# Reciprocal square roots of the q/k norm on VectorE instead of POOL, and a later place for the gain on kT

## Chip, cores, metric

One core of one Trainium2 chip. The time is the device time of one execution in microseconds; the median of several executions is compared.

## What is computed

Attention with RMS-normalised q and k, then a two-layer feed-forward with SiLU. All is fp32.

```python
# q, k, v: (8, 12, 448, 64); g_q, g_k: (64,); w_in: (768, 2048); w_out: (2048, 768)
rms = np.sqrt(np.mean(x * x, axis=-1, keepdims=True) + 1e-06)   # of q and of k
q_n, k_n = q / rms(q) * g_q, k / rms(k) * g_k
scores = np.matmul(q_n, k_n.transpose(0, 1, 3, 2)) / np.sqrt(64)
attn = softmax(scores)
x = np.matmul(attn, v)          # (B, H, S, D) -> (B*S, H*D) = (3584, 768)
h = x @ w_in
out = (h / (1 + np.exp(-h))) @ w_out
```

## The kernel before

**Couples.** Two pairs of heads (four heads of one batch entry) make a couple; there are NC = 24, numbered c = 0 to 23, six to a group of two batch entries (GROUP = 6). Each couple has a `visit(c)` and then a `between(c)`. In `visit` TensorE computes scores (L695, tile sc), ScalarE takes their exponentials (L700), TensorE multiplies the weights of the couple before and of this one with v (L732, tile av), and VectorE divides by the row sums while it copies out of PSUM (L790). A small copy of a constant into a bank of av (L708, `turn`) stands between two runs of L732 and orders them; inside a visit it is once VectorE's and once ScalarE's.

**Filler.** In `between` TensorE works on the feed-forward's first product of an earlier group: `begin` sets up the work, and each of two calls of `fill` per couple takes 13 or 14 matmul steps from it. It is a Strassen-Winograd scheme (class `Seven`): seven products of three steps each; the results leave PSUM through two banks (tile mm). Products 2, 6, 7, 3 and 4 are added up on VectorE (L816), products 1 and 5 are copied by ScalarE (L866, L876), and two sums of SBUF tiles are POOL's (`u2 += p5` at L878, and L879). The SiLU (L996) and the save of a row to `hidden` (L891, on SyncE's queue) follow. `fill` also deals out other work between the steps: `others` spread evenly, and `prompt`, whose first piece is issued at once and each further one after three more steps.

**Norm of couples c = 6 to 23.** `sum_squares` squares q or k on ScalarE into the buffer `squares` (L649) and sums groups of 32 on VectorE (L650). `scale` adds the two halves of a row by a matmul with `ident` (L662), makes mean + epsilon on VectorE (L663), raises it to -1/2 on POOL (L670: 28 columns for q, 28 for k) and multiplies the rows by it on POOL (L674). Couple c + 2 is scaled at the end of `between(c)`; c = 7 at the start of `between(6)`, and c = 6 in two halves in `between(4)` and `visit(5)`. The scaled rows are turned by VectorE in `flip`, q at L634 and k at L637. After k's turn ScalarE multiplies kT by the gains (L638), and the k load of couple c + 2 is issued to SyncE's queue. Couples c = 0 to 5 are normalised in another way (class `Norm`, L476), which the change leaves alone.

**Order.** Every engine runs its instructions in the order in which the code issues them; nothing is re-ordered, and waits between engines follow from the data. In the second `fill` of a couple `prompt` is: the first half of the row sums' reciprocals (L775), then the second half with its spreading by six DMAs (L781, L783), then `sum_squares(c + 2, "q")`. `flip(c + 1, "k")`, with L637 and L638, is issued before that fill.

**Weights.** w_in is loaded in pieces on SyncE's queue (L84), split by ScalarE (L99, L100), rounded by VectorE (L122, L125, L129) and added on POOL (L133). A load waits until the buffer of an earlier piece has been read by L133. Couples up to c = 10 do this beside everything else. VectorE also forms sums of w_in there (L813, L816).

**End.** After couple 23 the last group's feed-forward and the second product run (lines from L1165 on, tile alone).

Of the kernel before, what the change touches and what calls it, by code (L numbers as in the profile page):

```python
# [12 lines left out]
AF = mybir.ActivationFunctionType  # L13
ALU = mybir.AluOpType
AX = mybir.AxisListType
I32 = mybir.dt.int32
# [7 lines left out]


SCORE_MAX = 60.0

BANK = 512

# [160 lines left out]
def kernel(  # L190
# [161 lines left out]
    with tc.manual_schedule(), tc.tile_pool(  # L352
# [18 lines left out]
        for i in range(2):  # L371
# [9 lines left out]
        nc.vector.tensor_scalar(  # L381
            out=small, in0=most, scalar1=float(SCORE_MAX / D**0.5), scalar2=None, op0=ALU.is_le
        )
# [132 lines left out]
def bounded(  # L516
# [3 lines left out]
    P, D, R, J, S = z.P, z.D, z.R, z.J, z.S  # L520
# [6 lines left out]
    NC, loads, place, norm, spare, ones, first, squares = (  # L527
        own[name] for name in ("NC", "loads", "place", "norm", "spare", "ones", "first", "squares")
    )
    GROUP = z.NPAIR  # L530
# [13 lines left out]
    def piece(n):  # L544
        nonlocal at
        at += n
        return work[:, at - n : at]

    qT = piece(2 * S).rearrange("p (i s) -> p i s", i=2)
    kT = piece(z.NK)  # L550
# [13 lines left out]
    n = 2 * room.COLS  # L564
# [13 lines left out]
    def q_of(c):  # L578
        return rows_q[c % 2 if c < GROUP else 0]

    def load_q(c):

        if 0 < c < NC:
            loads["q"](c, raw_of(c) if c < GROUP else q_of(c))
# [32 lines left out]
    def transpose_k(c):  # L617


        assert z.KB == BANK  # L620
        t = ps.tile([P, 2, BANK], F32, name="sc", bufs=2)
        rows = place[f"k{c % 2}"]
        for i in range(2):
            for j in range(z.KEYS + 1 - i):
                nc.tensor.transpose(t[:, i, ts(j, P)], rows[:, ds((z.KA, z.KB)[i] + j * P, P)], ident)
        columns = t.rearrange("p i s -> p (i s)")[:, 0 : z.NK]
        nc.scalar.activation(kT, columns, AF.Copy, scale=gains)
        if c + 2 < NC:
            loads["k"](c + 2)

    def flip(c, name):

        if name == "q":
            nc.vector.transpose(qT.rearrange("p i s -> p (i s)"), q_of(c)[:, 0 : z.NK])  # L634
            load_q(c + 1)
            return
        nc.vector.transpose(kT, place[f"k{c % 2}"])  # L637
        nc.scalar.activation(kT, kT, AF.Copy, scale=gains)  # L638
        if c + 2 < NC:
            loads["k"](c + 2)  # L640

    n = z.NK // z.Q

# [11 lines left out]
    def scale(c, names="qk"):  # L655

        if c >= NC:
            return
        start = "qk".index(names[0]) * n
        f = norm.rms[c % 2][:, ds(start, len(names) * n)]  # L660
        t = ps.tile([P, 2, BANK], F32, name="sc", bufs=2)[:, 0, 0 : len(names) * n]
        nc.tensor.matmul(t, ident, f, start=True, stop=True)  # L662
        nc.vector.tensor_scalar(  # L663
            out=f, in0=t, scalar1=1.0 / D, scalar2=1e-6, op0=ALU.mult, op1=ALU.add
        )
        for i, name in enumerate(names):
            rows = q_of(c)[:, 0 : z.NK] if name == "q" else place[f"k{c % 2}"]
            rows = rows.rearrange("p (n e) -> p n e", e=z.Q)
            factor = f[:, ts(i, n)]
            nc.gpsimd.tensor_tensor(  # L670
                out=factor, in0=factor, in1=minus_half.to_broadcast([P, n]), op=ALU.pow
            )
            factor = factor.rearrange("p (n one) -> p n one", one=1).to_broadcast([P, n, z.Q])
            nc.gpsimd.tensor_tensor(out=rows, in0=rows, in1=factor, op=ALU.mult)  # L674

# [74 lines left out]
    def sum_up(c):  # L750

        n = D // 2
        early = c < GROUP
        t = bank(S) if early else ps.tile([P, 2, BANK], F32, name="sc", bufs=2)[:, 0, 0:S]
        terms = [(0, lambda: weights(c, 0))]
        if early:
            terms = [(0, lambda: weights(c, LEFT - 1))] + terms + [(1, None)]  # L760
        for k, (which, w) in enumerate(terms):
            if k == len(terms) - 2:
                yield
            for h in range(2):
                for i in range(2):
                    nc.tensor.matmul(  # L766
                        t[ds(h * D + i * n, n), :],
                        ones[:, which + i if which else 0],
                        eleft[:, h] if which else w()[:, i, h],
                        start=(k == 0), stop=(k == len(terms) - 1),  # L770
                    )

        def invert(half):
            rows = ts(half, S // 2)
            nc.vector.reciprocal(out=r[0][:, rows], in_=t[:, rows])  # L775

        def spread():
            mine = [a.rearrange("(h i p) s -> i h p s", h=2, i=2) for a in r]
            for i in range(2):
                for h in range(2):  # L780
                    nc.sync.dma_start(mine[1][i, h], mine[0][1, h])  # L781
            for h in range(2):
                nc.sync.dma_start(mine[0][1, h], mine[0][0, h])  # L783

        yield [lambda: invert(0), lambda: (invert(1), spread())]

    def divide(c, source):
        for i in range(2):
            x = x_of(c, i)
            nc.vector.tensor_tensor(  # L790
                out=x, in0=x if source is None else source[i], in1=r[i], op=ALU.mult
            )
# [136 lines left out]
    def sum_x(group, c):  # L929
        right_sums(*quarters(group, c), *sums_of_x(c))  # L930
# [128 lines left out]
    def take(n, *which):  # L1059

        for i in which or range(len(regions)):
            a, at = regions[i]
            if at + n <= a.shape[1]:
                regions[i][1] += n
                return a[:, ds(at, n)]
        raise AssertionError
# [10 lines left out]
    for at in ((1, 2), (2, 1), (2, 2)):  # L1077
        a = take(2 * z.HALF)
        results[at] = [a[:, ts(t, z.HALF)] for t in range(2)]
    a = take(2 * z.HALF)  # L1080
# [205 lines left out]
    def begin(work, columns, parts):  # L1286
        finish()
        filler.update(work=work, due=0.0, share=columns / parts)
# [31 lines left out]
    def finish():  # L1320
        run(filler["work"])
# [26 lines left out]
    def last_two(c):  # L1348
        return [c // GROUP * 2 - 2, c // GROUP * 2 - 1]

    def visit(c):
# [40 lines left out]
        if c == GROUP - 1:  # L1392
            scale(c + 1, "q")
# [18 lines left out]
    def run_all(work):  # L1412
        for piece in work:
            piece()

    def between(c):

        def transposes_and_sums():
            summing = sum_up(c)
            if c < GROUP:  # L1420
                next(summing)
            if c == GROUP:
                flip(c + 1, "q")
            if c < GROUP - 1:
                transpose_k(c + 1)
            elif c < NC - 1:
                flip(c + 1, "k")
            reciprocals = next(summing)
            if GROUP // 2 <= c <= EARLY:
                divide(c - 1, None)  # L1430
            return reciprocals

        if c < GROUP - 1:
            transpose_q(c + 1)
        elif c == GROUP:
            scale(c + 1)
        elif c < NC - 1:
            flip(c + 1, "q")
        if c < GROUP // 2:
            inverting.extend(transposes_and_sums())  # L1440
        elif c == GROUP - 1:
            run_all(transposes_and_sums())
        if c >= GROUP and c % GROUP == 0:
            fetched = range(AHEAD) if c == GROUP else ()
            columns = products - 2 * HW * S * len(fetched)
            work = halves_in(last_two(c), range(HF), plain_in, dict(begun), fetched)
            begin(work, columns, 2 * GROUP)
            begun.clear()
        late = add(c, LEFT - 1) + add(c, LEFT) if c >= GROUP else []
        keys = [lambda: sum_squares(c + 2, "k")] if c >= GROUP - 2 else []  # L1450
        queries = [lambda: sum_squares(c + 2, "q")] if c >= GROUP else []
        fill(late + weights_in(c, 0) + keys)
        prompt = transposes_and_sums() if GROUP // 2 <= c != GROUP - 1 else []
        if c == GROUP // 2:
            begin(make_ahead([0, 1]), AHEAD * 2 * HW * S, GROUP - 1)
        fill(weights_in(c, 1), prompt + queries)
        if c == GROUP - 2:
            pair_up()
            scale(c + 2, "k")
        elif c >= GROUP:  # L1460
            scale(c + 2)
        if c % GROUP == GROUP - 1:
            finish()
            if c == GROUP - 1:
                begun[0] = fetch_ahead([0, 1], 0)
            else:
                sum_x([c // GROUP * 2, c // GROUP * 2 + 1], 0)
        if GROUP <= c < NC - 1:

            nc.scalar.activation(first, minus_half, AF.Exp)  # L1470
        if c == NC - 1:
            while rounder.load():
                pass
# [236 lines left out]
```

## Time and profile before

| | |
|---|---|
| median of 3 runs | 1369.82 us (1369.28 to 1370.48) |
| profiled execution | 1367.72 us, of it 1365.9 us span |
| granted TensorE clock, mean | 0.989 |
| TensorE matmuls busy | 1301.1 us (95%) |
| VectorE busy | 956.5 us (70%) |
| ScalarE busy | 476.3 us (35%) |
| POOL busy | 445.5 us (33%) |

The profile is of one execution; its time lies 2.1 us below the median. In the views PE is TensorE, PEld its weight load, DVE VectorE, ACT ScalarE, POOL GpSimd, SPq SyncE's DMA queue. In a timeline a line gives start and duration in microseconds, the engine, the line of code, the operation, output<-input, the count, and in brackets how long the engine had been idle and what ended it. A group's line gives busy time, mean ns of one, and idle time with its releaser. A line of the waits view gives the waiting engine and line, what it waited for, then the total, the count and the longest.

### The profile page before, as it was taken

The page shows a single profiled execution, that of the slowest core. Times are in us where ns is not written, and L with a number is a line of the kernel's source. Part 1 is how long each engine was busy: PE and PEld are TensorE (multiplying, and loading weights), DVE is VectorE, ACT ScalarE, POOL GpSimd, SP SyncE. Part 2 cuts the span into 40 slices and gives each one's busy share as a digit, 9 for nine tenths or more (in the row PEclk, how much of TensorE's full clock was granted, in tenths as well). Part 3 has the DMA queues.
Part 4 walks back from the last instruction along what each step waited for, and adds up shares of the span by engine and source line. Part 5 has one row for each costly group of instructions (what it writes and reads, how often), then busy time and mean ns, then how long its engine had stood idle before and what let it go on. Part 6 is the DMA issues. An engine that isn't in the chain of part 4 may idle for free.

```text
span 1365.9 us, 19539 instructions
## 1 busy us (share of the span) xinstructions
PE 1301.1 (95%) x7113; PEld 818.2 (60%) x7113; DVE 956.5 (70%) x1595; ACT 476.3 (35%) x859; POOL 445.5 (33%) x241
## 2 busy tenths in 40 slices
PE   8997798888999999999999999999999999999998
PEld 4332343343444444444444455556999999999998
DVE  5785776675765555765554677679887787878785
ACT  7865263453544454444454234420000000000000
POOL 6755556554544544544542134330000000000000
PEclk9999999899999999999999999999999999999999
DMA  9564253522433343433331247531413232323311
GB/s 243 145 158 98 69 147 84 154 70 65 105 78 78 78 105 78 106 78 75 78 94 47 99 131 235 188 120 43 128 45 126 73 97 74 102 78 99 114 57 38
DMA packets 252558, 139.42 MB, mean 102 GB/s; under 512 B 190436, under 2 KB 236388, under 8 KB 252452
## 3 DMA queue, kind: packets, MB, share of 16 engines
q1 hardware_dynamic: 251888, 137.09, 35.9%
q8 instruction: 58, 0.95, 0.3%
q0 software_dynamic: 256, 0.79, 0.2%
q14 instruction: 48, 0.39, 0.1%
q10 hardware_dynamic: 308, 0.20, 0.1%
HBM read 88.47 MB, written 41.29 MB: 95 GB/s over the span
## 4 chain that ended last, share of the span: by engine, by line
PE 80%; DVE 7%; issue 4%; ACT 3%; DMA 2%; POOL 2%; SPq 1%; ACTq 0%; DVEq 0%; POOLq 0%
PE mm L858 23%; PE alone L1165 22%; PE sc L695 8%; PE av L732 8%; PE mm L1165 7%; PE alone L858 7%; PE alone L1202 2%; DVE work L746 2%; DVE work L775 1%; PE sc L766 1%; SPq L249 1%; ACT stage L996 1%; POOL rms L670 1%; PE mm L1202 1%; DVE rms L650 1%
## 5 line engine op out<-in xcount | busy, mean ns | idle before, releaser
L858 PE MATMUL mm<-x,W 128*128 128x448 f32 x636 | 262.7, 556 | 23.4 <-ACT stage L876 11.1
L858 PEld LDWEIGHTS mm<-x,W 128*128 128x128 f32 x636 | 118.1, 192 | 159.5 <-issue 114.0
L670 POOL TENSOR_TENSOR rms<-rms,minus_half 128x28 f32<-128x28 f32 x36 | 176.3, 4896 | 96.5 <-DVE rms L663 96.5
L858 PE MATMUL mm<-sums_x,W 128*128 128x448 f32 x456 | 190.2, 555 | 17.7 <-DVE stage L816 14.2
L746 DVE TENSOR_TENSOR work<-work 128x896 f32<-128x896 f32 (+1 forms) x114 | 138.8, 1242 | 46.6 <-PE av L732 46.1
L695 PE MATMUL sc<-work 64*64 64x448 f32 x1344 | 159.7, 543 | 1.2 <-ACT work L700 1.1
L732 PE MATMUL av<-work,rows 64*64 64x448 f32 x1296 | 148.6, 539 | 8.3 <-DVE x L790 2.7
L700 ACT ACTIVATE work<-sc 128x448 f32<-128x448 f32 x252 | 120.9, 542 | 97.4 <-PE sc L695 85.4
L858 PEld LDWEIGHTS mm<-sums_x,W 128*128 128x128 f32 x456 | 85.3, 193 | 115.7 <-issue 80.5
L503 POOL DMA_DIRECT2D out_dram<-x x2 | 1.3, 653 | 443.2 <-DVE x L816 443.2
L1165 PE MATMUL alone<-W,rows 128*128 128x192 f32 x608 | 113.0, 326 | 0.0
L878 POOL TENSOR_TENSOR parts<-parts,stage 128x448 f32<-128x448 f32 x31 | 42.0, 1356 | 209.8 <-DVE parts L816 209.8
L732 PEld LDWEIGHTS av<-work,rows 64*64 64x64 f32 x1296 | 53.0, 133 | 84.1 <-issue 37.2
L1165 PEld LDWEIGHTS alone<-W,rows 128*128 128x128 f32 x608 | 101.2, 190 | 0.0
L695 PEld LDWEIGHTS sc<-work 64*64 64x64 f32 x1344 | 51.5, 133 | 70.0 <-issue 34.1
L1165 PE MATMUL alone<-W,work 128*128 128x192 f32 x382 | 72.2, 326 | 0.0
L650 DVE TENSOR_REDUCE rms<-rows 128x28 f32<-128x896 f32 x36 | 38.7, 1076 | 44.3 <-ACT rows L649 44.2
L996 ACT ACTIVATE stage<-stage 128x896 f32<-128x896 f32 x63 | 57.2, 945 | 31.3 <-DVE stage L816 30.6
L674 POOL TENSOR_TENSOR rows<-rows,rms 128x896 f32<-128x896 f32 x36 | 64.4, 1790 | 2.8
L1165 PEld LDWEIGHTS alone<-W,work 128*128 128x128 f32 x382 | 63.8, 190 | 0.0
L1175 ACT COPY rows<-alone 128x192 f32<-128x192 f32 x34 | 10.8, 318 | 136.9 <-PE alone L1165 78.7
L775 DVE RECIPROCAL work<-sc 128x224 f32<-128x224 f32 x36 | 55.1, 1533 | 1.0 <-PE sc L766 1.0
(244 smaller groups left out, 2135.9 us busy)
## 6 DMA issues: line engine op xcount, KB each, us to landing
hidden<-stage SPq DMA_DIRECT2D x63, 448.0 KB, 2.8
work<-hidden SPq DMA_DIRECT2D x21, 1024.0 KB, 5.1
rows<-in_moe_w_out_dram SPq DMA_DIRECT2D x32, 384.0 KB, 3.4
W<-in_moe_w_in_dram SPq DMA_DIRECT2D x22, 512.0 KB, 5.0
work<-work SPq DMA_DIRECT2D x144, 56.0 KB, 1.9
rows<-in_q_dram SPq DMA_DIRECT2D x144, 56.0 KB, 2.2
rows<-in_k_dram SPq DMA_DIRECT2D x144, 56.0 KB, 2.2
x<-hidden SPq DMA_DIRECT2D x7, 1024.0 KB, 5.5
```

The costliest lines, as they stand in the source:

```text
L650: nc.vector.tensor_reduce(out=norm.rms[c % 2][:, ts("qk".index(name), n)], in_=squares.rearrange("p (n e) -> p n e", e=z.Q), axis=AX.X, op ...
L670: nc.gpsimd.tensor_tensor(out=factor, in0=factor, in1=minus_half.to_broadcast([P, n]), op=ALU.pow)
L674: nc.gpsimd.tensor_tensor(out=rows, in0=rows, in1=factor, op=ALU.mult)
L695: nc.tensor.matmul(two[ds(half * D, D), h, 0:S], keys[rows, ts(half, D)], qT[rows, pair, :], start=True, stop=True,)
L700: nc.scalar.activation(eleft[:, h] if j == LEFT else weights(c, j)[:, i, h], two[:, h, 0:S], AF.Exp, scale=norm.column(c, i, h, j) if c < ...
L732: nc.tensor.matmul(sums[i][ds(h * D, D), :], v, w, start=(j == 0 and step == 1), stop=(j == LEFT - 1 and step == 1),)
L746: nc.vector.tensor_tensor(out=total, in0=total, in1=more, op=ALU.add)
L775: nc.vector.reciprocal(out=r[0][:, rows], in_=t[:, rows])
L858: nc.tensor.matmul(t, self.left(name, s), self.right(name, s), start=s == ends[0], stop=s == ends[1])
L878: nc.gpsimd.tensor_tensor(out=u2, in0=u2, in1=p5, op=ALU.add)
L996: nc.scalar.activation(t, t, AF.Silu)
L1165: nc.tensor.matmul(t, x[:, i], y, start=i == ORDER[0], stop=i == ORDER[-1])
```

## The change

After L663, ten VectorE instructions compute the reciprocal square root in place: a start value from the bits of the number (one tensor_scalar on int32 views) and three Newton steps of three instructions each, with two stretches of `squares` as scratch. The two pows on POOL go; the two multiplications of the rows stay. The gain on kT is taken out of `flip` and becomes a piece of its own, the third of the prompt list, so that `sum_squares(c + 2, "q")` becomes the fourth. At c = 5 the list is issued as a whole, at once.

```diff
+RSQRT_START = float(0x5F375A86)
...
         nc.vector.transpose(kT, place[f"k{c % 2}"])
-        nc.scalar.activation(kT, kT, AF.Copy, scale=gains)
         if c + 2 < NC:
             loads["k"](c + 2)
+
+    def gain():
+
+        nc.scalar.activation(kT, kT, AF.Copy, scale=gains)
...
             out=f, in0=t, scalar1=1.0 / D, scalar2=1e-6, op0=ALU.mult, op1=ALU.add
         )
+        y, a = (squares[:, ts(i, len(names) * n)] for i in range(2))
+        nc.vector.tensor_scalar(
+            out=y.bitcast(I32), in0=f.bitcast(I32), scalar1=-0.5, scalar2=RSQRT_START,
+            op0=ALU.mult, op1=ALU.add,
+        )
+        for i in range(3):
+            nc.vector.tensor_tensor(out=a, in0=f, in1=y, op=ALU.mult)
+            nc.vector.scalar_tensor_tensor(
+                out=a, in0=a, scalar=-0.5, in1=y, op0=ALU.mult, op1=ALU.mult
+            )
+            nc.vector.scalar_tensor_tensor(
+                out=f if i == 2 else y, in0=a, scalar=1.5, in1=y, op0=ALU.add, op1=ALU.mult
+            )
         for i, name in enumerate(names):
...
-            nc.gpsimd.tensor_tensor(
-                out=factor, in0=factor, in1=minus_half.to_broadcast([P, n]), op=ALU.pow
-            )
             factor = factor.rearrange("p (n one) -> p n one", one=1).to_broadcast([P, n, z.Q])
             nc.gpsimd.tensor_tensor(out=rows, in0=rows, in1=factor, op=ALU.mult)
...
             reciprocals = next(summing)
+            if GROUP - 1 <= c < NC - 1:
+                reciprocals.insert(2, gain)
```

## The prediction

> **What bounds the kernel now.** I read the page first (busy shares), then the windows view by stage, TensorE's timeline for its gaps, and for each gap the timelines of the engines that it waited for.
>
> ```profile
> PE 1301.1 (95%) x7113; PEld 818.2 (60%) x7113; DVE 956.5 (70%) x1595; ACT 476.3 (35%) x859; POOL 445.5 (33%) x241
> ...
> L670 POOL TENSOR_TENSOR rms<-rms,minus_half 128x28 f32<-128x28 f32 x36 | 176.3, 4896 | 96.5 <-DVE rms L663 96.5
> ```
>
> TensorE is the bound over the whole span; POOL's pow (L670) is its largest single group, 4.9 us for 28 columns. Whether POOL ever holds TensorE is a matter of stage, so I cut the span (columns: us, then busy PE, PEld, DVE, ACT, POOL, then granted clock, DMA share, GB/s):
>
> ```profile
> 140.00:250.00 110.00, 90.28 (x425) 39.68 (x424) 76.86 (x94) 47.07 (x76) 61.75 (x27) 0.92 0.43 109
> 250.00:350.00 100.00, 89.69 (x493) 39.97 (x493) 70.81 (x83) 46.21 (x81) 57.12 (x23) 0.98 0.34 81
> 350.00:450.00 100.00, 97.54 (x524) 43.20 (x523) 62.50 (x76) 47.21 (x78) 48.37 (x19) 1.00 0.35 86
> ```
>
> From 350 us on TensorE is 98% busy at full clock: there little can be won. From 140 to 350 us (c = 6 to 11, the couples that still round w_in on VectorE and POOL) it is idle for 19.7 + 10.3 = 30 us, and the clock drops too. After 800 us no changed instruction runs. TensorE's timeline names the gaps:
>
> ```profile
> 162.23 4.19 PE L858 MATMUL mm<-sums_x,W 128*128 128x448 f32 x6 [6.71 <-DVE stage L816]
> ...
> 242.53 4.85 PE L858 MATMUL mm<-x,W 128*128 128x448 f32 x6 [7.88 <-ACT stage L876]
> ...
> 290.18 1.77 PE L858 MATMUL mm<-sums_x,W 128*128 128x448 f32 x4 [3.00 <-DVE stage L816]
> ...
> 321.61 6.47 PE L858 MATMUL mm<-sums_x,W 128*128 128x448 f32 x12 [2.05 <-ACT stage L866]
> ```
>
> The six matmuls after the two long gaps take 4.19 and 4.85 us where six take 2.42 elsewhere: a long gap costs about 2 us more in clock. For the first gap, POOL's timeline:
>
> ```profile
> 145.90 5.62 POOL L670 TENSOR_TENSOR rms<-rms,minus_half 128x28 f32<-128x28 f32 x1 [14.36 <-DVE rms L663]
> 151.60 1.88 POOL L674 TENSOR_TENSOR rows<-rows,rms 128x896 f32<-128x896 f32 x1
> 153.44 5.23 POOL L670 TENSOR_TENSOR rms<-rms,minus_half 128x28 f32<-128x28 f32 x1
> 158.74 1.70 POOL L674 TENSOR_TENSOR rows<-rows,rms 128x896 f32<-128x896 f32 x1
> 160.39 1.13 POOL L878 TENSOR_TENSOR parts<-parts,stage 128x448 f32<-128x448 f32 x1
> ```
>
> L878 (u2 += p5) had its inputs at 151.1 and stood behind the normalisation until 160.4; VectorE's L816 waited for it until 161.56 ("7.53 <-POOL parts L878") and TensorE for L816. The second gap is the same queue one step removed: POOL's rounding add L133 stood behind pow until 224.03, and SyncE's load of w_in behind L133:
>
> ```profile
> SPq L84 <- POOL W L133: 40.0, 4, 19.6
> ```
>
> SyncE stood until 226.19; with it the v and q loads and the save of the hidden row (issued 239.11), whose landing L876 waited for until 241.95. The other two gaps are ScalarE's and VectorE's order: L638 (the gain on kT) waits on L637, and copies out of PSUM stand behind it:
>
> ```profile
> ACT work L638 <- DVE work L637: 92.7, 18, 15.3
> ```
>
> At 321 us L866 ran at 321.04, directly after L638, some 2 us after its product was done.
>
> **What the Trainium skill says.** "VectorE: DVE Perf Modes", TRN2 errata, gives fp32 tensor_tensor (N+151)/0.96 ns. The trace agrees: 691 ns by formula for 128x512 (rows 681 to 691), 624 for 448 (L790 624). "GPSIMD Engine Reference", Key points: POOL contends with VectorE instructions that run in a two-port mode or have two SBUF inputs. Here L125 took 1.80 us beside L674 (427 ns alone) and L746 2.13 (1.09 alone), but L816 with a PSUM operand 0.58 to 0.62 beside L674. "TensorE: Matmul & The Clock Gate", Part 1, has the array fall to half clock after some 3.4 us idle: the 4.19 and 4.85 us above fit. No row of this trace shows a 56-column tensor_tensor.
>
> **Part 1: pow out of POOL.** 36 pows go, 176.3 us, 9.8 us per couple. On VectorE come 10 instructions after each of the 19 L663. With 56 columns: the tensor_scalar about 0.19 us (L472, 8 to 14 columns, 0.171), nine others (56+151)/0.96 = 0.216 us, 2.13 us busy; all depend on the one before, and dependent pairs here start 0.035 us after the end (L122 231.03+0.43, L125 231.50), so the chain is 2.48 us. The two 28-column calls: 2.2 us. VectorE's load rises by 17 x 2.13 + 2 x 1.85 = 40 us. Bounds for one instruction: 0.171 (L472) to 0.35 (128x192 rows): chain 2.1 to 3.9 us.
>
> Where it lies: in 16 couples (visits 7 to 22) the chain falls between L663 and L708, the write into an av bank that TensorE needs next:
>
> ```profile
> 399.48 0.22 DVE L663 TENSOR_SCALAR rms<-sc 128x56 f32<-128x56 f32 x1 [0.23 <-PE sc L662]
> 401.95 0.16 DVE L708 COPY av<-minus_half 128x1 f32<-128x1 f32 x1 [2.25 <-PE av L732]
> ```
>
> VectorE is idle there for 2.25 us. The weight load behind L708 starts at 402.16 and its matmul at 402.43, back to back with the scores ahead of it, so 0.14 us more are free: 2.39 against 2.48, 0.1 us late, x 16 = 1.6 us. L790 behind L708 waits for TensorE until 403.45 and is not moved; it has one SBUF operand, so L674, now beside it, should leave it alone. At c = 7 and 11, POOL still runs L878/L879 beside the chain: about 0.9 us each, 1.8 us. POOL then scales q 4.3 us after L663 instead of 6.6, and k after 6.0 instead of 13.1; the transposes L634 and L637, 10 to 20 us later, don't notice, except at c = 5 (L634 waited 1.59 us: gain 1.6). The scratch y, a is in `squares`: its next Square is a fill later (at c = 6, 148.97, when the chain ends at about 148.4).
>
> Gains, gap by gap:
> - c = 6 (142 to 175). The chain delays the first evacuation (146.74) by 2.5 us, and TensorE's next product with it. L674 ends at about 152 instead of 160.3, the evacuation of product 7 at about 155, L878 at 156.2, L816 at 157.3; TensorE goes on at 158.5 instead of 162.23 and keeps its clock: 3.7 + 1.8 = 5.5 us. With the 1.6 us above: 7.1.
> - c = 8 (210 to 255). L674 ends at 216.6, so L125 is done at 217.05, L129 at 217.8, L133 at 219.1 instead of 226.1: SyncE goes on 6.9 us earlier, the row's save is issued at about 232.3 and landed at 235.2; TensorE runs dry at 234.6. The gap shrinks from 7.88 to about 1.2: 6.7, clock 2.4, and most of 0.47 + 0.81 (L746 beside L133): 9.5 us.
> - c = 9, 10: 0.60 at 268 (L746 beside L674), 1.22 and 1.63 at 309 and 313 (L133 and L878 behind pow): 3.4 us.
>
> **Part 2: the gain moved.** One ScalarE instruction, 1.04 us, no DMA. It goes from just after L637 to the sixth matmul step of the second fill; the k load (8 DMAs on SyncE) stays directly behind L637, so that queue isn't touched. Scores need kT some 5 us after that (step 14), so it is hidden; at c = 5 nothing of ScalarE lies between old and new place. It passes L99/L100, L866 or L876, and the silus. What it pushes: the Square of q and its reduce L650 go from step 6 to step 9, on VectorE past one evacuation. TensorE's L662 needs L650 at step 13 or 14, 3 us later, and Square plus L650 take 2.1: hidden.
> - c = 10: the 2.05 at 321 and its slow clock (6.47 against 4.67 for 12): 3.5 us.
> - c = 9: at 290 L816 stood behind L650, which waited for Square: 3.0. c = 7: p5's copy behind the gain, 0.6 of 1.21. c = 6: p5's copy behind Square, 1.05.
> - c = 14, 17, 20 (430.71, 534.05, 638.30): the same L816 behind L650, 0.78 each: 2.3.
>
> Sum: 7.1 + 9.5 + 3.4 + 3.5 + 3.0 + 0.6 + 1.05 + 2.3 = 30.5 us. Against it 1.6 + 1.8, and one term that I choose: per couple c = 7 to 10 VectorE is busy 27 to 30 us of the 33 that a couple takes without gaps (c = 11: 32.8), and goes to over 90%, so a fifth of the 26 us won before 350 us is likely to come back as other waits: 5. Net 22 us. From the profiled 1367.7 (span 1365.9 and 1.8 around it) that is 1345.7; the median is 2.1 higher, so 1348.
>
> **The rivals.**
> - *Slower: the chain outlasts VectorE's gap ahead of L708.* Its price is (chain - 2.39) in 16 couples. It eats 26 us from a chain of 4.0 us, 0.40 us an instruction. For it: every instruction depends on the last, none of this size is in the trace, and POOL may stretch them. Against: formula and rows put it at 2.5. At 0.45: 16 x 2.1 = 34 less 26, 1378. Chance 0.10.
> - *Cover elsewhere: VectorE becomes the bound in c = 6 to 11.* POOL's L674 and L133 now fall into VectorE's busy stretches, and the w_in stalls return as L816 waits; only the c = 8 gap and half the rest go: about 10 us, 1360. Chance 0.20.
> - *No change*, gains and late L708 cancelling (chain near 3.5 to 4): 0.05.
> - *Forecast*: 0.65, 1338 to 1356.
>
> I count 0.2% (2.7 us) as what a measurement here can tell from no change. Faster 0.85, same 0.05, slower 0.10. The range 1336 to 1364 takes in the forecast and the second rival, and leaves out the rest.
>
> **What would show it.** Right: no L670 rows; ten VectorE rows of about 0.2 us a call; SyncE's L84 wait on L133 far under 40 us; gaps at about 158 and 235 under 3 us; clock in 140:250 near 1.0; L708 waits under 0.3 us each. Wrong: TensorE's av waits on L708 of a us or more per couple, or the stage from 140 to 350 us as long as before.

## The result, and the profile after

| | before | changed |
|---|---|---|
| median | 1369.66 us (1369.28 to 1371.83, six runs) | 1363.72 us (1362.40 to 1364.75, six runs) |
| profiled execution, span | 1367.72, 1365.9 us | 1364.28, 1362.5 us |

The ratio is 0.9953, interval 0.994 to 0.9966: 5.9 us faster, where 22 were forecast. Of the runs told below one, of the kernel with the gain alone, took 1528.04 us at a mean granted clock of 0.844 where its five others had 0.991 or more; it is left out of that kernel's ratio, and the median told below, 1361.16, would be 1360.20 without it.

Lines below are the changed kernel's unless another kernel is named; they have moved on by 5 to 15. L663 is now L668, the chain is L672 to L681, POOL's multiplication L674 is L689, L708 is L723, L732 is L747, L746 is L761, L790 is L805, L813 is L828, L816 is L831, L858 is L873, L866 and L876 are L881 and L891.

The page of the changed kernel, its line of busy times and the group of POOL's multiplications:

```profile
PE 1302.9 (96%) x7113; PEld 818.6 (60%) x7113; DVE 991.2 (73%) x1785; ACT 475.7 (35%) x859; POOL 266.2 (20%) x205
...
L689 POOL TENSOR_TENSOR rows<-rows,rms 128x896 f32<-128x896 f32 x36 | 62.7, 1762 | 143.9 <-ACT work L715 49.2
```

POOL has lost 179 us and 36 instructions, VectorE has gained 35 us and 190: the change did what it says. The windows of the changed kernel, with the columns of the prediction's table:

```profile
140.00:250.00 110.00, 100.30 (x500) 43.48 (x494) 90.27 (x143) 53.59 (x88) 33.03 (x23) 0.96 0.48 125
250.00:350.00 100.00, 93.85 (x490) 42.05 (x486) 79.12 (x108) 47.64 (x80) 25.43 (x18) 1.00 0.35 81
350.00:450.00 100.00, 94.23 (x510) 41.77 (x502) 66.50 (x103) 44.41 (x75) 18.51 (x12) 0.98 0.33 82
```

From 140 to 350 us TensorE is busy for 14 us more than before, and the clock has risen from 0.92 and 0.98 to 0.96 and 1.00. But the third row, where it had been 97.54 busy at full clock, has lost 3.3 us and some clock. The gaps of TensorE's timeline say why:

```profile
150.88 4.78 PE L873 MATMUL mm<-x,W 128*128 128x448 f32 x12 [0.85 <-DVE parts L831]
157.13 1.02 PE L873 MATMUL mm<-sums_x,W 128*128 128x448 f32 x2 [1.47 <-DVE parts L831]
...
165.74 4.22 PE L873 MATMUL mm<-sums_x,W 128*128 128x448 f32 x6 [2.41 <-DVE stage L831]
...
233.70 4.13 PE L873 MATMUL mm<-x,W 128*128 128x448 f32 x6 [2.56 <-ACT stage L891]
...
357.63 1.77 PE L747 MATMUL av<-work,rows 64*64 64x448 f32 x8 [5.11 <-DVE av L723]
...
569.96 1.77 PE L747 MATMUL av<-work,rows 64*64 64x448 f32 x8 [5.21 <-DVE av L723]
571.51 3.21 PE L710 MATMUL sc<-work 64*64 64x448 f32 x16
```

At c = 8 the 7.88 us of before have become 2.56. At c = 6 the gap of 6.71 us is gone from its place, but three waits of 0.85, 1.47 and 2.41 us stand elsewhere in the couple. Two gaps of over 5 us are new, and each takes clock with it: eight av matmuls take 1.77 us behind it and 0.98 in the kernel before, sixteen score matmuls 3.21 and 1.85. Both gaps lie at the entry of a visit that follows a group's last couple (c = 12 and 18), and there VectorE's queue looks like this:

```profile
352.01 0.62 DVE L831 TENSOR_TENSOR stage<-mm,parts 128x448 f32<-128x448 f32 x1
352.54 1.86 DVE L828 TENSOR_TENSOR sums_x<-x 128x448 f32<-128x448 f32 x1
354.43 2.00 DVE L828 TENSOR_TENSOR sums_x<-x,sums_x 128x448 f32<-128x448 f32 x1
356.35 0.61 DVE L828 TENSOR_TENSOR x<-x 128x448 f32<-128x448 f32 x1
356.89 0.61 DVE L828 TENSOR_TENSOR sums_x<-x,sums_x 128x448 f32<-128x448 f32 x1
357.42 0.15 DVE L723 COPY av<-minus_half 128x1 f32<-128x1 f32 x1
```

At 352.01 the chain has just ended. At c = 11 and 17 the code issues, behind `scale`, the last copy of a product out of PSUM (an evacuation, L831) and four sums of x (`sum_x` of part 0), and only then L723. No instruction there waits: VectorE is simply full. The two L828 of 1.86 and 2.00 us run beside POOL:

```profile
352.22 3.73 POOL L689 TENSOR_TENSOR rows<-rows,rms 128x896 f32<-128x896 f32 x2 [4.51 <-issue]
```

The same place in the timeline of the kernel before:

```profile
365.14 0.61 DVE L816 TENSOR_TENSOR stage<-mm,parts 128x448 f32<-128x448 f32 x1
365.67 0.61 DVE L813 TENSOR_TENSOR sums_x<-x 128x448 f32<-128x448 f32 x1
...
367.93 0.15 DVE L708 COPY av<-minus_half 128x1 f32<-128x1 f32 x1
```

L708 is over at 368.08, and TensorE's next av matmul starts at 368.14: it was just in time, with nothing to spare.

### The profile page after: what moved, and what is told of

Same layout as the page of the kernel before. It is cut to its first block, busy times and chain, and to the rows that moved or that the text cites. A ratio compares the mean times of both kernels' runs of the same rounds, so it can differ in the third digit from the quotient of the medians.

```text
span 1362.5 us, 19714 instructions
## 1 busy us (share of the span) xinstructions
PE 1302.9 (96%) x7113; PEld 818.6 (60%) x7113; DVE 991.2 (73%) x1785; ACT 475.7 (35%) x859; POOL 266.2 (20%) x205
## 4 chain that ended last, share of the span: by engine, by line
PE 64%; DVE 2%; DMA 1%; SPq 1%; ACT 1%; issue 0%; POOL 0%; ACTq 0%; DVEq 0%; POOLq 0%
PE alone L1180 22%; PE mm L873 17%; PE mm L1180 7%; PE alone L873 7%; PE sc L710 4%; PE av L747 4%; PE alone L1217 2%; PE mm L1217 1%; PE sc L781 1%; DVE sums_x L828 0%; DMA hidden<-stage 0%; SPq L251 0%; DVE work L831 0%; DMA work<-work 0%; POOL parts L893 0%
## 5 line engine op out<-in xcount | busy, mean ns | idle before, releaser
L873 PE MATMUL mm<-x,W 128*128 128x448 f32 x636 | 258.6, 549 | 13.8 <-ACT stage L891 5.2
L873 PEld LDWEIGHTS mm<-x,W 128*128 128x128 f32 x636 | 117.6, 191 | 147.5 <-issue 111.9
L873 PE MATMUL mm<-sums_x,W 128*128 128x448 f32 x456 | 187.2, 549 | 7.4 <-DVE stage L831 4.4
L747 PE MATMUL av<-work,rows 64*64 64x448 f32 x1296 | 152.1, 552 | 20.9 <-DVE av L723 15.4
L710 PE MATMUL sc<-work 64*64 64x448 f32 x1344 | 163.7, 558 | 2.2 <-ACT work L715 2.0
L761 DVE TENSOR_TENSOR work<-work 128x896 f32<-128x896 f32 (+1 forms) x114 | 128.6, 1153 | 51.1 <-PE av L747 46.0
L873 PEld LDWEIGHTS mm<-sums_x,W 128*128 128x128 f32 x456 | 84.9, 191 | 102.3 <-issue 80.9
L747 PEld LDWEIGHTS av<-work,rows 64*64 64x64 f32 x1296 | 53.0, 135 | 98.2 <-issue 39.4
L689 POOL TENSOR_TENSOR rows<-rows,rms 128x896 f32<-128x896 f32 x36 | 62.7, 1762 | 143.9 <-ACT work L715 49.2
L881 ACT COPY stage<-mm 128x448 f32<-128x448 f32 x27 | 14.3, 531 | 130.2 <-PE mm L873 130.1
L790 DVE RECIPROCAL work<-sc 128x224 f32<-128x224 f32 x36 | 55.1, 1533 | 1.0 <-PE sc L781 1.0
```

Of the source, the lines that this page charges most:

```text
L710: nc.tensor.matmul(two[ds(half * D, D), h, 0:S], keys[rows, ts(half, D)], qT[rows, pair, :], start=True, stop=True,)
L747: nc.tensor.matmul(sums[i][ds(h * D, D), :], v, w, start=(j == 0 and step == 1), stop=(j == LEFT - 1 and step == 1),)
L761: nc.vector.tensor_tensor(out=total, in0=total, in1=more, op=ALU.add)
L873: nc.tensor.matmul(t, self.left(name, s), self.right(name, s), start=s == ends[0], stop=s == ends[1])
```

## Where the time went, couple by couple

TensorE's row-sum matmul (L662 before, L667 after) marks the end of a couple. The table gives the change of each stretch's length against the kernel before, in us, read from one profiled execution of each kernel. The forecast's column is its own steps put in their places, ahead of its discount of 5. The last three kernels are experiments told below.

| stretch | forecast | changed | gain moved only | Newton only | chain in the visit |
|---|---|---|---|---|---|
| up to c = 6 | -1.6 | +2.7 | +2.2 | -1.5 | -1.5 |
| c = 6 | -6.6 | -3.7 | -2.9 | -3.1 | -3.7 |
| c = 7 | +0.4 | -1.4 | +0.8 | +2.8 | -0.2 |
| c = 8 | -9.4 | -6.4 | -0.6 | -6.5 | -5.7 |
| c = 9 | -3.5 | -4.3 | -3.3 | -0.8 | -4.3 |
| c = 10 | -6.2 | -3.1 | -2.1 | -0.7 | -3.1 |
| c = 11 | +1.0 | +0.6 | 0.0 | +0.6 | +0.6 |
| c = 12 | +0.1 | **+5.8** | 0.0 | **+5.7** | +2.3 |
| c = 13 to 17 | -1.1 | -1.1 | -1.3 | -0.1 | -1.3 |
| c = 18 | +0.1 | **+7.2** | 0.0 | **+6.6** | +2.3 |
| c = 19 to 21 | -0.5 | -0.7 | -0.7 | -0.2 | -0.8 |
| sum | -27.3 | -4.5 | -7.8 | +2.9 | -15.3 |

Up to c = 12 the changed kernel and the last one issue the same instructions, and yet the first row differs by 4.2 us: that much the early part varies from one execution to another, and it is no effect of an edit. A difference of a us in one cell of c = 6 to 8 is no more than that either (c = 7: -1.4 and -0.2 with the same instructions). From c = 6 to 11 the changed kernel gained 18.3 us; the forecast had 24.3 there less its discount, 19. What the forecast did not have are the 13.0 us of c = 12 and 18.

## The experiments

Every ratio is against the kernel before, timed on the same chip with the kernel named; medians move by a us or two between chips, so ratios are compared.

**Each part alone.** One kernel moves the gain and leaves pow on POOL (the two edits are shown against the changed kernel):

```diff
+            nc.gpsimd.tensor_tensor(
+                out=factor, in0=factor, in1=minus_half.to_broadcast([P, n]), op=ALU.pow
+            )
...
-        y, a = (squares[:, ts(i, len(names) * n)] for i in range(2))
-        nc.vector.tensor_scalar(
...
```

> Only the later place of the gain; the reciprocal square root stays POOL's pow. Theory A (the change's lost time sits at the two group ends, c = 12 and 18, where the chain and POOL's multiplications now hold L723 behind four sum_x; the gain's move is nearly free): 6 to 10 us faster than before, from the gaps at 290 (3.0), 321 (3.5) and the three of 0.78, with L84 still waiting 40 us on L133 and no new wait on L723. Theory B (the gain's move does little, the c = 6 to 11 gains all come from POOL): under 3 us.

The other has the chain on VectorE and leaves the gain behind the turn:

```diff
         nc.vector.transpose(kT, place[f"k{c % 2}"])
+        nc.scalar.activation(kT, kT, AF.Copy, scale=gains)
...
-            if GROUP - 1 <= c < NC - 1:
-                reciprocals.insert(2, gain)
```

> Only the chain on VectorE in place of pow; the gain stays directly behind L639. Theory A: the gaps at 162 and 242 shrink by 3 to 6 us each, and 10 to 13 us are lost at c = 12 and 18 (L723 waits of about 5 us): within 3 us of before. Theory B: faster by 4 us or more, about what the whole change won (5.9).

The gain's move alone took 1361.16 us against 1368.57, ratio 0.9946 (0.9931 to 0.9961). It alone is worth what the whole change brought. The chain alone took 1372.04 against the same 1368.57, ratio 1.0031 (1.0021 to 1.0042): the part that clears POOL made the kernel slower. Its TensorE timeline at c = 12:

```profile
364.05 1.77 PE L745 MATMUL av<-work,rows 64*64 64x448 f32 x8 [5.12 <-DVE av L721]
```

With the gain alone there is no gap at c = 12 or 18 (the table). So the loss belongs to the chain's part. The effects of the two parts roughly add up: by the table -7.8 and +2.9 against -4.5, by the ratios -7.4 and +4.2 against -6.4, where the difference of 3 us is as wide as the three intervals together allow.

**Taking the loss away.** Two kernels change only the group ends. One issues POOL's two multiplications of couples 13 and 19 behind the next visit's division:

```diff
+        if c % GROUP == 1 and c > GROUP + 1:
+            return
+        multiply(c, names)
...
         if c == GROUP - 1:
             scale(c + 1, "q")
+        if c > GROUP and c % GROUP == 0:
+            multiply(c + 1)
```

> The changed kernel, with only POOL's two multiplications of c = 13 and 19 put behind the division of the next visit; the chain stays ahead of the four sum_x. If POOL's contention with sum_x makes a good half of the wait on L723 there: the wait falls from 5.1 to about 2.5 us twice, and the time is 4 to 6 us under the changed kernel (ratio to before 0.991 to 0.993). If the chain's own 2.5 us make nearly all of it: under 2 us gained.

It took 1361.53 us, ratio 0.9946 (0.9934 to 0.9959). That looks like 1 us or so gained, but its POOL timeline shows that the edit moved nothing:

```profile
350.82 3.73 POOL L699 TENSOR_TENSOR rows<-rows,rms 128x896 f32<-128x896 f32 x2 [4.52 <-issue]
```

The chain ended at 350.7 there. POOL has its own order, nothing of POOL's stood between the old and the new place, and no data of VectorE's later work is asked for; so the multiplications began where they had begun, and the gap at c = 12 was 5.12 us. The run tells nothing of the two causes. The other kernel issues the chain there too, only the mean (L668) staying behind:

```diff
                 divide(c - 1, sums)
                 run_all(beside[1:2])
+                if c > GROUP and c % GROUP == 0:
+                    root(c + 1)
```

`root` is the chain and the two multiplications; `scale` leaves it out for these two couples:

```diff
+        if c % GROUP == 1 and c > GROUP + 1:
+            return
+        root(c, names)
```

> The changed kernel, with chain and multiplications of c = 13 and 19 put behind the division of the next visit. Theory A: L723 is on time at c = 12 and 18, and 10 to 13 us come back, less what the chain costs behind the division: ratio to before 0.986 to 0.989 (1350 to 1354). Rival (the lost time is spread over all couples, as late L723 or VectorE as the bound in c = 6 to 11): within 3 us of the changed kernel.

It took 1355.05 us, ratio 0.99 (0.9885 to 0.9916), 13.5 us under the kernel before and faster than both kernels. In its VectorE timeline the four sums are unstretched and L723 (here L733) follows them at once. The last of them, and L733:

```profile
349.52 0.62 DVE L838 TENSOR_TENSOR sums_x<-x,sums_x 128x448 f32<-128x448 f32 x1
350.05 0.15 DVE L733 COPY av<-minus_half 128x1 f32<-128x1 f32 x1
```

and TensorE goes on at 350.26. The gain is 3.5 us at c = 12 and 5.0 at c = 18 of the table, not the whole loss, because something else is late next in the same couple:

```profile
364.81 2.52 PE L883 MATMUL mm<-sums_x,W 128*128 128x448 f32 x6 [1.69 <-ACT stage L891]
```

**How much is the chain, how much POOL's multiplication.** Both kernels start from the one with the gain alone. The first adds a chain whose result nobody reads, with pow and so the multiplications where they were:

```diff
+        y, a = (squares[:, ts(i, len(names) * n)] for i in range(2))
+        nc.vector.tensor_scalar(out=y.bitcast(I32), in0=f.bitcast(I32), ...)
+        for i in range(3):
+            nc.vector.tensor_tensor(out=a, in0=y, in1=y, op=ALU.mult)
...
```

> The kernel with the gain moved and the power kept on POOL, plus ten VectorE instructions of the chain's kinds and sizes at the chain's place, whose result nobody reads. It adds the chain's length to VectorE's queue; POOL's multiplications stay where the power puts them, some ten us later than in the changed kernel. Theory A (at the two group ends the late L723 has two equal halves: the chain's own 2.5 us, and two L828 that POOL's multiplications stretch by 1.3 us each): L723 is 2.2 to 2.6 us late at couples 12 and 18, no L828 is stretched, and the time is 5 to 8 us above the kernel with the gain alone (1361), so 1366 to 1369. Theory B (the chain lies in idle time of VectorE there too, and the multiplications make the whole 5 us): L723 in time at both ends, 1361 to 1363.

The second multiplies the rows of couples 13 and 19 by one ahead of the pow, with no chain:

```diff
+        if c % GROUP == 1 and c > GROUP + 1:
+            one = squares[:, 0:1]
+            nc.vector.tensor_scalar(out=one, in0=f[:, 0:1], scalar1=0.0, scalar2=1.0, ...)
+            for rows in (q_of(c)[:, 0 : z.NK], place[f"k{c % 2}"]):
...
+                nc.gpsimd.tensor_tensor(out=rows, in0=rows, in1=factor, op=ALU.mult)
```

> The kernel with the gain moved and the power kept on POOL; for couples 13 and 19 alone, POOL first multiplies q and k by one (in the same form as L689, 3.7 us in all, the ones written by one small VectorE instruction behind L668), so that it runs beside the L828 of the group ends. No chain. Theory A: two L828 take 1.8 to 2.1 us in place of 0.62, L723 is 2.3 to 2.9 us late at couples 12 and 18, and the time is 4 to 6 us above the kernel with the gain alone (1361): 1365 to 1367. Theory C (the multiplications matter only behind a chain that has already used up the slack): the stretched L828 are hidden, L723 less than 1 us late, 1361 to 1362.5.

The chain in vain took 1370.01 us against 1370.18, ratio 1.0001 (0.9991 to 1.0012), 7.5 us above the gain alone by the ratios; couples 12 and 18 are 5.6 us of that in its profile (3.5 and 2.0, measured as in the table). Its TensorE timeline at c = 12, and its VectorE timeline there:

```profile
368.93 0.98 PE L750 MATMUL av<-work,rows 64*64 64x448 f32 x8 [2.49 <-DVE av L726]
369.96 3.26 PE L713 MATMUL sc<-work 64*64 64x448 f32 x16
```

```profile
366.46 0.62 DVE L831 TENSOR_TENSOR sums_x<-x 128x448 f32<-128x448 f32 x1
367.11 0.62 DVE L831 TENSOR_TENSOR sums_x<-x,sums_x 128x448 f32<-128x448 f32 x1
```

The sums are not stretched, and the gap is the chain's own 2.5 us; it is 2.49 at c = 18 too. The multiplication by one took 1368.87, ratio 0.9986 (0.9977 to 0.9996), 5.5 us above the gain alone; couples 12 and 18 are longer by 2.5 and 3.7 us. Its TensorE timeline at c = 12 and 18, and its VectorE timeline at c = 12:

```profile
366.57 0.98 PE L746 MATMUL av<-work,rows 64*64 64x448 f32 x8 [2.82 <-DVE av L722]
...
575.54 1.02 PE L746 MATMUL av<-work,rows 64*64 64x448 f32 x8 [2.82 <-DVE av L722]
576.34 3.21 PE L709 MATMUL sc<-work 64*64 64x448 f32 x16
```

```profile
361.49 1.82 DVE L827 TENSOR_TENSOR sums_x<-x 128x448 f32<-128x448 f32 x1
363.35 1.98 DVE L827 TENSOR_TENSOR sums_x<-x,sums_x 128x448 f32<-128x448 f32 x1
```

Without any chain, the stretched sums make a gap of 2.82 us, about 0.2 of it the small instruction that writes the ones. 2.49 + 2.82 = 5.31, against 5.11 and 5.21 in the changed kernel: the two halves add up, and there was no slack for either. Theory A holds in both runs, B and C fall. Each half also took clock at one of its two places: the sixteen score matmuls behind the gap took 3.26 us at c = 12 of the first kernel and 3.21 at c = 18 of the second, where they take 1.85 in the kernel before; at the other place of each they took 1.85 and 1.68.

**Do the parts add up without the loss?** The kernel with the chain in the visit, but with the gain back behind the turn (the diff of the second kernel above on top of the fourth):

> The kernel with the chain and the multiplications of couples 13 and 19 behind the next visit's division, but with the gain where it was before, right behind L639. Theory A (the gain's move and the chain are worth their parts and add up): the gain move is worth 7 to 9 us, so this kernel is 7 to 9 us above 1355, at 1362 to 1364, some 4 to 7 us under the kernel before. Theory D (the gain's move only pays because the chain brings the next k earlier): 1355 to 1358.

1364.65 us against 1370.18, ratio 0.9958 (0.9939 to 0.9976). Against 0.99 with the gain moved, the move is worth 7.9 us, about as much as alone (7.4): the gain's move does not need the chain, and theory D falls.

**Another repair, and what is late next.** The chain stays, the four sums go behind the next visit's division:

```diff
-                    for i in range(0 if c == GROUP else 1, HW):
+                    for i in range(HW):
                         sum_x(last_two(c), i)
...
-            else:
+            elif c == NC - 1:
                 sum_x([c // GROUP * 2, c // GROUP * 2 + 1], 0)
```

> The changed kernel with the four sums of x that stand between the chain and L723 at the two group ends moved into the next visit, behind the division; the chain stays where the change put it. Theory A (the time at the group ends is lost by what stands ahead of L723, whichever of it is taken away): L723 is at most 0.8 us late at couples 12 and 18, a wait of 1 to 2.5 us comes later in these couples as in the kernel with the chain in the visit, and the time is 7 to 9 us under the changed kernel, 1355 to 1358, ratio 0.989 to 0.992. Rival (the chain itself has to leave that place): L723 still 2 to 3 us late, 1360 to 1363.

1355.06 us against 1370.01, ratio 0.989 (0.9873 to 0.9907), the same as with the chain moved. TensorE waits only 0.23 us for L723 at c = 12. But the evacuation L831 still stands behind the chain (350.01), the SiLU behind L831, and on ScalarE the table load and the exponentials behind the SiLU. ScalarE's timeline, then TensorE's:

```profile
350.66 0.95 ACT L1011 ACTIVATE stage<-stage 128x896 f32<-128x896 f32 x1 [4.01 <-DVE stage L831]
351.63 1.28 ACT L1487 ACT_TABLE_LOAD   x1
```

```profile
354.05 2.33 PE L710 MATMUL sc<-work 64*64 64x448 f32 x16 [2.31 <-ACT work L715]
```

So the chain delayed two things at the group ends; the second was hidden under L723's wait. Next I tried to remove what was left in the kernel with the chain in the visit, by moving the last four sums of that visit behind the first L761 (its L771):

```diff
         run_all(add(c, 1))
+        if c > GROUP and c % GROUP == 0:
+            sum_x(last_two(c), HW - 1)
```

> The kernel with the chain and the multiplications of couples 13 and 19 behind the next visit's division (1355), and the last four sums of x of the visits 12 and 18 behind L761's first pair. Theory A (what is left at the group ends, 1.69 us before the second product at couple 12, is VectorE's queue in that visit: eight L828, two of them stretched to 2.0 and 2.1 us, ahead of L761): the wait goes, 1.5 to 2.3 us at each end, so 1350.5 to 1352.5. Theory E (it only moves on to the q transposition L636 and to the flip of k behind it, 2.2 us later): 1354 to 1357.

1357.66 us against 1370.18, ratio 0.9909 (0.9892 to 0.9927): no gain over 0.99. The 1.69 us behind the first twelve matmuls went, and a longer wait came six matmuls (one product) later. VectorE's and TensorE's timelines:

```profile
363.78 1.10 DVE L636 STREAM_TRANSPOSE work<-rows 128x896 f32<-128x896 f32 x1
364.81 2.05 DVE L771 TENSOR_TENSOR work<-work 128x896 f32<-128x896 f32 x2
366.78 0.62 DVE L841 TENSOR_TENSOR stage<-mm,stage 128x448 f32<-128x448 f32 x1
```

```profile
367.45 4.12 PE L883 MATMUL mm<-sums_x,W 128*128 128x448 f32 x6 [2.47 <-DVE stage L841]
```

The evacuation at 366.78 now stands behind sums, turn and adds, and the clock falls after the gap (4.12 for six matmuls). As theory E had it, the wait only moved on; of the two places tried in that couple neither was free.

**Couple 6.** The kernel with the chain in the visit, and couple 7's `scale` issued in visit 6 ahead of the division instead of in the middle of couple 6:

```diff
+                if c == GROUP:
+                    scale(c + 1)
                 divide(c - 1, sums)
...
-        elif c == GROUP:
-            scale(c + 1)
```

> The kernel with the chains of couples 13 and 19 in the visit (1355), and the mean, chain and multiplications of couple 7 issued in visit 6 ahead of its division, where VectorE waits 3.8 us for the spread of the reciprocals, in place of the middle of couple 6. Theory A (couple 6 got 3.7 us in place of the forecast 6.5 because the chain, 2.5 us, and POOL's multiplications, which stretch three L761 from 3.2 to 5.7 us, stand ahead of the evacuations that TensorE waits for): the gap of 2.5 us at the second product of couple 6 goes; 2 to 4 us less, 1351 to 1353. Rival (twelve L828 behind the division are stretched instead, and the adds come late all the same): within 1.5 us of 1355.

1352.92 us against 1370.01, ratio 0.9869 (0.985 to 0.9888); the interval just meets that of 0.99, so it is the fastest seen, but how much it gains is open. The gap of 2.53 us behind the first twelve matmuls of couple 6 became 0.63 and 1.34 in two pieces. The stretched instruction moved. In the kernel with the chain in the visit three adds took

```profile
148.29 5.67 DVE L771 TENSOR_TENSOR work<-work 128x896 f32<-128x896 f32 x3
```

and in this one three adds are whole, but the sums are not:

```profile
138.84 2.00 DVE L838 TENSOR_TENSOR sums_x<-x,sums_x 128x448 f32<-128x448 f32 x1
...
149.90 3.20 DVE L771 TENSOR_TENSOR work<-work 128x896 f32<-128x896 f32 x3
```

Part of A and part of the rival. That chain and multiplications ahead of the evacuations cost something in couple 6 is shown; the size of it isn't.

**The chain in every visit.** All chains from couple 8 on behind the division:

```diff
-        if c % GROUP == 1 and c > GROUP + 1:
+        if c > GROUP + 1:
             return
...
-                if c > GROUP and c % GROUP == 0:
+                if c > GROUP:
                     root(c + 1)
```

> The kernel with the chains of couples 13 and 19 in the visit (1355), with the chains and multiplications of all couples from 8 in the visit ahead, behind the division. Theory A (what the chain costs in the other couples is the lateness of L723: 1.2 us at couple 7, 0.4 at 11, about 0.1 in the others): 2 to 3 us less, 1352 to 1353.5. Rival (POOL's multiplications then fall beside L761's adds in every couple, which stretches two of them by 1.3 us each, and TensorE or ScalarE waits for these adds): 1355 to 1365.

1378.38 us against 1370.01, ratio 1.006 (1.0045 to 1.0075): slower than before the change, and beyond what either theory gave. The rival had the mechanism, stretched instructions of VectorE, and not its reach. At visit 13 two L771 take 3.55 us for 2.09, as it said. But at visit 7 POOL's multiplications meet the sums of w_in (0.95 us each alone) ahead of the adds:

```profile
182.27 5.57 DVE L838 TENSOR_TENSOR W<-W 128x768 f32<-128x768 f32 x3
```

The adds end late, and TensorE stands and then runs slow (4.78 us for twelve elsewhere):

```profile
191.43 7.82 PE L883 MATMUL mm<-x,W 128*128 128x448 f32 x12 [3.69 <-DVE stage L841]
```

So taken over the ordinary couples the place between L668 and L723, which the change uses, is the better one of the two.

## Why the prediction was right or wrong, point by point

- **Sign: right; the range held by 0.3 us.** Faster, and 1363.72 lies inside 1336 to 1364, but no step spoke for the size that came: that it is inside is luck.
- **The chain's price: right.** Its instructions took 0.19 and 0.217 us; the formula that the Trainium skill gives ("VectorE: DVE Perf Modes", TRN2 errata) has 0.216, and the trace now has the 56-column row that was missing. The first rival (0.40 us an instruction) falls.
- **"In 16 couples (visits 7 to 22) the chain falls between L663 and L708 ... 0.1 us late": the step that failed.** It took c = 13 as the pattern for all. There it was even better than forecast: the chain ends, L723 runs at 392.27, and TensorE doesn't wait, so the 1.6 us were not paid. At c = 12 and 18 five instructions stood in that place already and the idle 2.25 us did not exist. Each us put there was a us lost, and two things were put there: the chain (2.49) and, through POOL, the multiplications (2.82). Together they made gaps of 5.11 and 5.21 us, behind which the clock fell: from the first matmul behind the gap to the second batch of score matmuls it took 4.59 us at c = 12 and 5.94 at c = 18, where the kernel before took 3.45 and 3.46. With a small wait later in the couple gone (0.46 us), that makes the 5.8 and 7.2 us of the table; 0.2 were forecast for both. How much clock such a gap takes did not repeat: the half gaps took from none to 1.5 us.
- **"L674, now beside it, should leave it alone": asked of the wrong instruction.** It was asked of L790, with one SBUF operand, and held there. Without the pow the first multiplication starts 2.8 us behind L668 instead of some 5, and the chain pushes the L828, with two SBUF operands, back to just that time. The page that the prediction quoted ("GPSIMD Engine Reference", Key points) has the two engines contend then; what was missing was to go through VectorE's queue at each place where POOL's work would newly lie.
- **c = 6: mis-sized,** -3.7 for -6.6. L674 now runs beside L746, 5.67 us for three adds, in the same stretch as the chain, and VectorE has no pause from 141.8 to 169.1 us: the wait for POOL is gone, and three waits for VectorE came (0.85, 1.47, 2.41).
- **The second rival (VectorE the bound in c = 6 to 11, 1360): right in part, near by luck.** Its mechanism is what c = 6 shows, but these couples still gave 18.3 us where it left about ten, and what brought the time near its 1360 was lost at c = 12 and 18.
- **c = 8: mechanism right, size off,** -6.4 for -9.4. SyncE's wait for the rounding add fell, and its load came 6.6 us earlier in the couple (6.9 were forecast):

```profile
SPq L86 <- POOL W L135: 27.9, 4, 14.7
```

  It was 40.0 and 19.6. The row had landed 25.6 us into the couple, as forecast (25.2). But the small waits ahead (0.47 and 0.81), which the forecast booked as a gain of their own (its 9.5 holds 0.4 for them; "most of" the two would have made it about 10), only let TensorE run dry 1.0 us sooner and wait longer for the same landing: the gap shrank from 7.88 to 2.56 instead of 1.2. Behind it six matmuls still took 4.13 us. The prediction's figure of some 3.4 us of idle time is no lower bound here: the clock was slow behind 2.56 us, and behind 2.05 in the kernel before.
- **c = 9 right, c = 10 half.** At c = 10 the 2.05 us and its slow clock went with the gain's move. The waits of 1.22 and 1.63 us that were put down to pow went only in part, to 0.76 and 1.07, and with the gain alone they stay as they were: POOL's pow was about a third of them. A third wait is new, with the gain alone too (1.65): one product behind the place of the 2.05, for an evacuation behind two reciprocals of VectorE.

```profile
299.56 2.52 PE L873 MATMUL mm<-x,W 128*128 128x448 f32 x6 [1.07 <-DVE stage L831]
...
309.32 2.52 PE L873 MATMUL mm<-sums_x,W 128*128 128x448 f32 x6 [1.64 <-DVE stage L831]
```

- **The three gaps of 0.78: right.** All gone, also with the gain alone. They lie at c = 13, 16 and 19, one couple earlier than the prediction counts them.
- **c = 7 and 11, "about 0.9 us each": half.** One chain instruction each was stretched, to 1.07 and 0.89 us; TensorE waited 0.56 and 0.39 us.
- **The discount** was the right size for c = 6 to 11 (18.3 measured, 19 forecast), and its reason, that other waits come back, is what c = 6, 8 and 10 show; the number itself was chosen, and that it fits is luck. The gain's move alone brought 8.0 us there, in sum, where 8.2 were forecast, so nearly all that came back came back from the chain's part. But the discount was meant for that stretch alone. It could not stand for a place at which nobody had looked. From 350 us on the forecast had booked no loss but the 0.1 us a couple: "there little can be won" was read, and that a stage 98% busy has much to lose was not.

## What to carry to other kernels

Before you put work into "the idle gap ahead of X", list every instance of X in the trace and read what stands ahead of it in each: the couples at a loop's seam are the exceptions, and they decided here. When a long instruction leaves one engine, what followed it there moves forward; look at what it newly runs beside. Try the parts of a change alone: here the part with the large story (-179 us of POOL) lost about 4 us by itself, the small one won 7.4, and moving the new work at two places of nineteen was worth another 7.

## What the runs showed of the hardware that was not expected

In these kernels POOL's pow did not disturb VectorE, POOL's multiplication did. In the kernel with the gain alone, VectorE's and POOL's timelines behind c = 12's division:

```profile
364.44 2.07 DVE L818 TENSOR_TENSOR sums_x<-x 128x448 f32<-128x448 f32 x1
366.54 0.62 DVE L818 TENSOR_TENSOR sums_x<-x,sums_x 128x448 f32<-128x448 f32 x1
367.08 0.62 DVE L818 TENSOR_TENSOR x<-x 128x448 f32<-128x448 f32 x1
```

```profile
364.33 1.70 POOL L679 TENSOR_TENSOR rows<-rows,rms 128x896 f32<-128x896 f32 x1
365.98 5.17 POOL L675 TENSOR_TENSOR rms<-rms,minus_half 128x28 f32<-128x28 f32 x1
```

The sum that starts beside the multiplication ends 0.5 us after it; those beside the pow take their plain 0.62. In the kernel before, 22 sums of this kind ran beside a pow alone and took 0.61 to 0.63 us. The Trainium skill ("SBUF — State Buffer", the section on the two separate sides) has the pair of ports that the two engines share locked for a whole instruction, against any GpSimd instruction that reads SBUF. The multiplication fits that; the pow reads SBUF as well, lasts 5.17 us and held nothing up, so here the measurement decides. Whether it is the operation or its few columns (28 against 896) no run here tells. Pow was expensive on POOL, but for VectorE it was a quiet neighbour, and its removal put a loud one into its place.
